# Local attention and a gated projection on one core: every engine's work put into one written list of 919 pieces

## Chip, core and metric

The kernel runs on one core of a Trainium2 chip. A core has a matrix engine (PE, whose weight loads are listed apart as PEld), a vector engine (DVE), a scalar engine (ACT), a GpSimd engine (POOL) and a queue that only issues transfers here (SP). Each engine takes its own instructions strictly in the order in which the program wrote them; between engines there are semaphores. The metric is the device time of one execution in microseconds (us); the span of a profile is the part of it from the first to the last instruction.

## What is computed

`reference` works on 4 batches, 8 heads, 768 positions and a head dimension of 64. It is float32 throughout.

```python
k_sum = k.reshape(B, H, 24, 32, D).max(axis=3)
v_sum = v.reshape(B, H, 24, 32, D).mean(axis=3)
scores_l = q @ k.T / 8, kept where |i - j| < 16
scores_s = q @ k_sum.T / 8 + log(32)
a = softmax(concat(scores_l, scores_s))
x = a @ concat(v, v_sum)                  # heads side by side: B, S, 512
gate = sigmoid(sum over k of conv_w[k] * x shifted by 4 - k)
out = (gate * (x @ w_val)) @ w_out
```

So a query sees 31 neighbours and 24 block summaries; a causal convolution of five taps gates the first 512 x 512 projection, and a second one follows. The three weights come in as 64-bit floats and are made into float32 on the chip.

## The kernel before

**Tiling.** There are 12 groups g of 256 positions (three to a batch) and 24 units u, two to a group, each with four heads. A unit runs through these stages, and the letters in brackets are those that the change uses: scores on PE (`mm_s`, s), mask and row minimum on DVE (`snorm`, n), exponentials and row sums on ACT (`exps`, e), reciprocal on DVE (r) and scaling on POOL (m, both in `norm`), transposes on PE (`tp`, t), their copy on ACT (`pcopy`, c), attention output on PE (`mm_x`, x), copies to SBUF on ACT and the float32 rest on POOL (`xout`: X and Y, Z), first tap on ACT (`ginit`, I), four more taps on DVE (`taps`, T), tanh on ACT (`gate`, G). Once for each group come the projections on PE (`val_mm`, v, and `out_mm`, o), with their evacuations: gating on DVE (gf), rounding on ACT (gh), rest on POOL (gl), output copy on ACT (ob) and store (O). From group 1 on the projections run as three passes, high and low parts of operand and weight; group 0 runs in one float32 pass straight from the tile `wf`, for which all four row blocks of a weight must be converted.

**Weights.** Each of the eight row blocks of `w_val` and `w_out` is converted by an ACT pass (L212, rb), a DVE shift (L220, sh) and a DVE shift-and-or (L221, or), then split by ACT (L252, wc) and POOL (L253, wl). Both weights pass through the one tile `wf`.

**Buffers.** PSUM holds one score buffer of two banks, one bank each for transposes, attention output and gate, and three banks of tag `pp` that projections and block summaries share. Queries have two tiles (`qbd`, L87 to 91), keys two tiles to each of four tags, `v` two tiles. Batch 0's raw values sit in key tiles.

**Order.** The schedule is manual: each engine's queue is the program text. Setup and units 0 to 7 are written out by hand (L611 to L791): two to three units of attention, then group 0's projection, and so on. From unit 8 on `step(s)` (L560) repeats one pattern: a projection, x of unit s-2, s and n of unit s, t of unit s-1, the exponentials, taps of unit s-2, a second projection. Loads are issued at fixed steps (`LOAD_K`, `LOAD_VT`, `early_loads`, `late_loads`); `fill_vs` (L193) copies block sums into a loaded `v` tile with four transfers.

Of the kernel before, what the change touches and what calls it, by code (L numbers as in the profile page):

```python
# [21 lines left out]
QT = 64  # L22
# [23 lines left out]
LOADS = "k0 q0 m k1 q1 n0 i k2 q2 n1 k3 q3 n2 n3 v0 c Q w0 w1 w2 w3 v1"  # L46
UPB = NTH * NHP
LOAD_K = {1: (2, 2, 4, 5)}
LOAD_VT = {1: (2, 2, 5, 6)}
PREP_K = {1: (-1,) * 4}  # L50
PREP_V = {1: (-1,) * 4}
DVE_V = ((1, 3),)
for _b in range(2, B):
    LOAD_K[_b] = tuple(_b * UPB + w for w in (-5, -4, -3, -2))
    LOAD_VT[_b] = LOAD_K[_b]
    PREP_K[_b] = tuple(_b * UPB + w for w in (-3, -2, -1, 0))
    PREP_V[_b] = tuple(_b * UPB + w for w in (-4, -3, -2, -1))
# [3 lines left out]
def tile_attention_then_gated_conv(  # L61
# [25 lines left out]
    NQB = 2  # L87
    qbd = []
    for i in range(NQB):
        t = cpool.tile([P, NPR, SG], F32, tag=f"qbd{i}", name=f"qbd{i}")  # L90
        qbd.append(t)
# [52 lines left out]
    def prep_v(b, pr):  # L144
        t = wk.tile([P, NB], F32, tag="vsT", name=f"vsT_{b}_{pr}", bufs=4)
# [80 lines left out]
    wraw = {}  # L226

    def load_w(nm, src, k, pool, tag):
        raw = pool.tile([P, 2 * DM if wide else DM], U32, tag=tag, name=f"raw_{nm}{k}")
        nc.sync.dma_start(raw, src[k * P : (k + 1) * P, :].bitcast(U32))  # L230
        wraw[nm, k] = raw

    wf = cpool.tile([P, 4, DM], F32, tag="wf", name="wf")

    scaled = {}

    def pre_w(nm, k):
        if wide:
            scaled[nm, k] = rebias(wraw[nm, k], DM, f"{nm}{k}", 2)

    def conv_w(nm, k):
        st = wf[:, k]
        raw = wraw.pop((nm, k))
        if wide:
            to_f32(st, raw, DM, f"{nm}{k}", 2, scaled.pop((nm, k), None))
        else:
            nc.vector.tensor_copy(st, raw.bitcast(F32))

    def split_w(nm, k):
# [29 lines left out]
    for a in LOADS.split():
        acts[a[0]](int(a[1]) if len(a) > 1 else 0)  # L280
# [6 lines left out]
    def group(g):  # L287
        if g not in grp:
            grp[g] = dict(
                xh=wk.tile([P, NPR, SG], F32R, tag="xh", name=f"xh_{g}") if g else None,  # L290
                xl=wk.tile([P, NPR, SG], F32R, tag="xl", name=f"xl_{g}") if g else None,
                gt=wk.tile([P, NPR, SG], F32, tag="gt", name=f"gt_{g}"),
                xf=wk.tile([P, NPR, HALO + SG], F32, tag="xf", name=f"xf_{g}"),
            )
            halo = grp[g]["xf"][:, :, :HALO]
            if g % NTH == 0:
                nc.gpsimd.memset(halo, 0.0)
            else:
                nc.gpsimd.tensor_scalar(
                    halo, grp[g - 1]["xf"][:, :, SG:], 1.0, 1.0, ALU.mult, ALU.mult  # L300
                )
        return grp[g]

    def mm_s(u, r):
        b, th, hp = units[u]
        g = b * NTH + th
        if r == 0:
            st[u] = dict(
                sp=ps_s.tile([P, 2, 512], F32, tag="s", name=f"s_{u}"),
                sn=wk.tile([P, NP, KW], F32, tag="sn", name=f"sn_{u}"),  # L310
                p=wk.tile([P, NP, KW], F32, tag="p", name=f"p_{u}", bufs=3),
                nm=wk.tile([P, NP], F32, tag="nm", name=f"nm_{u}", bufs=4),
                rs=wk.tile([P, NP], F32, tag="rs", name=f"rs_{u}", bufs=4),
            )
        pr = 2 * hp + r
        for j in range(TPU // 2):
            for e in range(2):
                for h in range(2):
# [4 lines left out]
                        st[u]["sp"][64 * e : 64 * e + 64, h, c * KW : c * KW + KW],  # L323
                        qbd[g % NQB][64 * h : 64 * h + 64, pr, i * QT : i * QT + QT],
# [5 lines left out]
    def snorm(u, r):  # L330
        b, th, hp = units[u]
        s = st[u]
        for j in range(TPU // 2):
            for h in range(2):
# [5 lines left out]
                    s["sn"][:, n, :],  # L340
                    s["sp"][:, h, c * KW : c * KW + KW],
# [5 lines left out]
                    s["nm"][:, n : n + 1],  # L347
                )

    def exps(u, r):  # L350
        s = st[u]
        for n in range(TPU * r, TPU * r + TPU):
            nc.scalar.activation(  # L353
                s["p"][:, n, :], s["sn"][:, n, :], AF.Exp, bias=s["nm"][:, n : n + 1],
                scale=-1.0, accum_out=s["rs"][:, n : n + 1],
            )

    def norm(u):
# [4 lines left out]
        for r in range(2):
            w = slice(TPU * r, TPU * r + TPU)
            nc.gpsimd.tensor_tensor(  # L365
                s["p"][:, w],
                s["p"][:, w],
                ri[:, w].unsqueeze(2).broadcast_to([P, TPU, KW]),
                ALU.mult,
            )  # L370
# [499 lines left out]
```

## Time and profile before

| | |
|---|---|
| runs, us | 262.33, 264.52, 330.56; median 264.52 |
| profiled span, us | 258.7 |
| span to the fastest run | 3.6 us lie around it |
| busy, us | PE 228.9, DVE 187.4, ACT 193.0, POOL 151.5 |
| first matmul starts, last one ends | 5.48, about 255.1 us |

Busy times overlap a little within an engine, as an instruction starts before the one ahead has quite ended, so the distance between starts is the better price of a piece. PE's sum is also swollen where it runs at the lower clock.

### The profile page before, as it was taken

What the parts mean: (1) busy time and instruction counts of PE and PEld (TensorE: products, weight loads), DVE (VectorE), ACT (ScalarE), POOL (GpSimd) and SP (SyncE); (2) the same over time, 40 slices, a digit from 0 to 9 for tenths busy, and PEclk for the clock granted to TensorE, in tenths of its full rate; (3) what the DMA queues carried; (4) which work ended last, traced back from release to release, by engine and by line L of the source; (5) the groups of instructions that cost most, each with busy time, mean ns of one, the idle gap of its engine ahead of it and who ended that gap; (6) DMA issues with size and microseconds to landing.
All of it is one profiled execution on the core that took longest, in us unless ns stands there. A gap on an engine that the chain in (4) does not pass through costs nothing.

```text
span 258.7 us, 7312 instructions
## 1 busy us (share of the span) xinstructions
PE 228.9 (88%) x2652; PEld 193.3 (75%) x2652; DVE 187.4 (72%) x691; ACT 193.0 (75%) x619; POOL 151.5 (59%) x212
## 2 busy tenths in 40 slices
PE   1258996997496979999999999999999999999994
PEld 1146785953392969888988988898889888988982
DVE  1856899999983877779777867987696669645610
ACT  1548997977829499888987898899879888976311
POOL 2243087769818297878664788897446634655130
PEclk9999999999977699999999999999999999999999
DMA  6999989284413968617118989172065323110122
GB/s 193 398 403 412 340 299 393 33 319 164 130 50 46 331 210 307 211 38 263 44 16 225 387 252 383 35 249 82 5 202 181 113 97 71 42 43 0 44 81 81
DMA packets 16884, 46.39 MB, mean 179 GB/s; under 512 B 2352, under 2 KB 3120, under 8 KB 16848
## 3 DMA queue, kind: packets, MB, share of 16 engines
q1 hardware_dynamic: 16848, 45.93, 51.7%
q8 instruction: 21, 0.34, 0.6%
q14 instruction: 15, 0.12, 0.2%
HBM read 37.46 MB, written 6.29 MB: 169 GB/s over the span
## 4 chain that ended last, share of the span: by engine, by line
PE 70%; DVE 13%; ACT 8%; POOL 3%; DMA 2%; issue 2%; SPq 1%; DVEq 0%; ACTq 0%; POOLq 0%
PE out L502 24%; PE val L464 21%; PE s L322 8%; PE x L398 8%; PE pt L378 8%; DVE g L439 5%; ACT p L353 4%; DVE sn L339 3%; DMA vT<-in_vT_dram 2%; DVE wf L221 1%; POOL p L365 1%; DVE wf L220 1%; DVE ks L129 1%; POOL wo L253 1%; ACT pts L382 1%
## 5 line engine op out<-in xcount | busy, mean ns | idle before, releaser
L439 DVE SCALAR_TENSOR_TENSOR g<-xf,cwt,g 128x256 f32<-128x256 f32 x192 | 93.9, 489 | 13.1 <-ACT g L430 6.0
L353 ACT ACTIVATE p<-sn,nm 128x120 f32<-128x120 f32 x192 | 73.3, 388 | 9.7 <-DVE nm L339 9.7
L365 POOL TENSOR_TENSOR p<-p,ri 128x480 f32<-128x480 f32 x48 | 47.0, 1001 | 41.2 <-DVE ri L362 37.6
L339 DVE CUSTOM_DVE_ANT_0 sn<-s,mask 128x120 f32<-128x120 f32 x192 | 40.9, 278 | 32.4 <-PE s L322 32.3
L464 PE MATMUL val<-xh,wv 128*128 128x256 f32 x352 | 51.1, 287 | 0.0
L502 PE MATMUL out<-wo,gh 128*128 128x512 f32 x176 | 46.8, 406 | 1.4 <-POOL wo L253 1.4
L464 PEld LDWEIGHTS val<-xh,wv 128*128 128x128 f32 x352 | 45.4, 191 | 0.3 <-issue 0.2
L322 PE MATMUL s<-k,qbd 64*64 64x120 f32 x768 | 28.9, 289 | 13.8 <-POOL k L139 11.1
L416 POOL TENSOR_TENSOR xl<-xf,xh 128x512 fp32r<-128x512 f32 x22 | 28.4, 1291 | 19.0 <-ACT xf L414 14.3
L378 PE MATMUL pt<-ident,p 128*120 128x128 f32 x192 | 31.6, 289 | 7.9 <-ACT pts L382 4.5
L502 PEld LDWEIGHTS out<-wo,gh 128*128 128x128 f32 x176 | 31.5, 188 | 8.5 <-POOL wo L253 2.1
L353 ACT ACTIVATION_READ_ACCUMULATOR p<-sn,nm 128x1 f32 x192 | 37.0, 193 | 0.0
L382 ACT COPY pts<-pt 120x512 f32<-120x512 f32 x48 | 27.6, 575 | 10.2 <-PE pt L378 10.2
L398 PEld LDWEIGHTS x<-pts,v 120*64 120x64 f32 x768 | 27.2, 141 | 10.1 <-issue 7.0
L322 PEld LDWEIGHTS s<-k,qbd 64*64 64x64 f32 x768 | 21.7, 143 | 17.4 <-POOL k L139 15.3
L487 POOL TENSOR_TENSOR gl<-gf,gh 128x512 fp32r<-128x512 f32 x22 | 28.5, 1298 | 7.9 <-ACT gh L478 7.9
L398 PE MATMUL x<-pts,v 120*64 120x64 f32 x768 | 31.2, 229 | 1.9 <-ACT pts L382 0.7
L378 PEld LDWEIGHTS pt<-ident,p 128*120 128x120 f32 x192 | 21.7, 142 | 14.4 <-POOL p L365 6.7
L447 ACT ACTIVATE gt<-g 128x512 f32<-128x512 f32 x24 | 14.3, 598 | 22.9 <-DVE g L439 22.9
L464 PE MATMUL val<-xl,wv 128*128 128x256 f32 x176 | 28.4, 283 | 0.0
L153 POOL TENSOR_TENSOR vT<-vT 128x384 f32<-128x384 f32 (+3 forms) x44 | 25.7, 584 | 2.6
L502 PE MATMUL out<-wo,gl 128*128 128x512 f32 x88 | 25.4, 409 | 0.7 <-POOL gl L487 0.7
(51 smaller groups left out, 270.3 us busy)
## 6 DMA issues: line engine op xcount, KB each, us to landing
v<-in_vw_dram SPq DMA_DIRECT2D x24, 512.0 KB
k<-in_kT_dram SPq DMA_DIRECT2D x16, 478.0 KB
vT<-in_vT_dram SPq DMA_DIRECT2D x16, 384.0 KB
out_dram<-ob SPq DMA_DIRECT2D x24, 256.0 KB
qbd<-in_qT_dram SPq DMA_DIRECT2D x11, 512.0 KB
raw_wv<-in_wv_dram SPq DMA_DIRECT2D x4, 512.0 KB
raw_wo<-in_wo_dram SPq DMA_DIRECT2D x4, 512.0 KB
v<-vs SPq DMA_DIRECT2D x36, 48.0 KB
```

What stands on the lines that cost most here:

```text
L322: nc.tensor.matmul(st[u]["sp"][64 * e : 64 * e + 64, h, c * KW : c * KW + KW], qbd[g % NQB][64 * h : 64 * h + 64, pr, i * QT : i * QT + QT ...
L339: nc.vector.tensor_tensor_reduce(s["sn"][:, n, :], s["sp"][:, h, c * KW : c * KW + KW], mask[:, mv, :], -1.0 / math.sqrt(D), 3.0e38, ALU.a ...
L353: nc.scalar.activation(s["p"][:, n, :], s["sn"][:, n, :], AF.Exp, bias=s["nm"][:, n : n + 1], scale=-1.0, accum_out=s["rs"][:, n : n + 1],)
L365: nc.gpsimd.tensor_tensor(s["p"][:, w], s["p"][:, w], ri[:, w].unsqueeze(2).broadcast_to([P, TPU, KW]), ALU.mult,)
L378: nc.tensor.transpose(s["pt"][:KW, i, :], s["p"][:, TPU * r + i, :], ident)
L382: nc.scalar.copy(s["pts"][:, TPU * r : TPU * r + TPU], s["pt"][:KW])
L398: nc.tensor.matmul(dst, v[:KW, i, c0 : c0 + D], src, start=True, stop=g > 0)
L416: nc.gpsimd.tensor_tensor(G["xl"][:, prs, :], x[:, prs, HALO:], G["xh"][:, prs, :].bitcast(F32), ALU.subtract)
L439: nc.vector.scalar_tensor_tensor(gt[:, r], x[:, pr, o : o + SG], cwt[:, pr, o : o + 1], gt[:, r], ALU.mult, ALU.add,)
L464: nc.tensor.matmul(pp[:, r], w, x, start=(n == 0), stop=(n == len(terms) - 1))
L487: nc.gpsimd.tensor_tensor(G["gl"][:, cos, :], gf, G["gh"][:, cos, :].bitcast(F32), ALU.subtract)
L502: nc.tensor.matmul(pp, x, w, start=(n == 0), stop=(n == len(terms) - 1))
```

## The change

The functions that issued several engines' work are cut up, so that each piece is one engine's work on one half unit, one projection half, one weight block or one transfer. The loops over steps and the hand-written beginning are gone; one list names all 919 pieces in program order, and each engine's queue is that list's part for it. No arithmetic changes and no instruction is added or dropped. Tile counts stay, except that the queries take their two tiles from the rotating pool, so a query load can take either tile once it is free. A projection of values is cut into halves r that can stand apart. `DVE_COPY` and `POOL_LOW` are empty. In the list, `s6.1` is unit 6, half 1; `v1.0.1` is group 1, pair 0, half 1; `Lk`, `Lq`, `Lv`, `Lu`, `Lwv`, `Lwo` are loads of keys, queries, values, transposed values and weight blocks, and F is `fill_vs`.

```diff
-LOADS = "k0 q0 m k1 q1 n0 i k2 q2 n1 k3 q3 n2 n3 v0 c Q w0 w1 w2 w3 v1"
-    LOAD_K[_b] = tuple(_b * UPB + w for w in (-5, -4, -3, -2))
...
+RAW_TAG = {'wv': ['gh', 'gl', 'gh', 'gl'], 'wo': ['gh', 'gl', 'xh', 'xl']}
+BUFS = {'p': 3, 'nm': 4, 'pts': 2, 'sn': 2, 'xh': 2, 'xl': 2, 'gt': 2, 'xf': 2, 'gf': 3, 'gh': 2, 'gl': 2, 'ob': 2, 'sc': 2, 'ks': 2, 'vsT': 4, 'rs': 4}
+ORDER = """
+Lk0.0 Lk0.1 ks0.0 ks0.1 Lp0 Lp1 Lc Lm Lk0.2 shc kc0.0 Lp2 kc0.1 s0.0 Lk0.3 Ln0 n0.0 e0.0 ks0.2
+kc0.2 cv s0.1 n0.1 ks0.3 s1.0 Lq1 Lp3 Ln2 e0.1 kc0.3 vp0.0 n1.0 Ln1 Li Ln3 s1.1 r0 vp0.1 Lwv2
+Lwv1 m0.0 vc0.1 n1.1 m0.1 e1.0 e1.1 rbc s2.0 vp2.1 s2.1 Lwv3 Lq2 vp1.0 vp1.1 Lk1.1 t0.0 n2.0
+Lk1.0 Lv0 Lwo3 Lu1.0 n2.1 s3.0 s3.1 c0.0 vp2.0 vp3.1 r1 n3.0 vp3.0 n3.1 shwv3 e2.0 e2.1 m1.1
+shwv2 m1.0 vc3.1 t0.1 c0.1 vc0.0 t1.1 vc1.0 s4.0 s4.1 hal0 vc2.1 vc3.0 vc2.0 vc1.1 rbwv3 r2
+rbwv2 e3.0 vb0 c1.1 vb1 orwv2 n4.0 n4.1 ks1.1 shwv1 ks1.0 m2.1 t1.0 vbc0 e3.1 Lv1 s5.0 vbc1 s5.1
+wcwv2 rbwv1 x0.0 x0.1 n5.1 orc orwv3 n5.0 orwv1 e4.0 Y0 c1.0 Lwv0 Lq3 r3 I0 T0.0 t2.1 e4.1 c2.1
+rbwv0 x1.0 m2.0 kc1.0 tv1.0 m3.0 kc1.1 x1.1 wcwv3 shwv0 r4 t2.0 s6.0 orwv0 c2.0 s6.1 t3.0 T0.1
+Lk1.2 Lu1.2 Lwo1 F1 Lwo2 Lk1.3 Y1 wlwv2 m3.1 Lv2 Lu1.3 rbwo3 c3.0 wcwv1 n6.0 Lq7 G0 ks1.2 I1
+v0.1.0 v0.0.0 x2.0 T1.0 ks1.3 x2.1 t3.1 e5.0 m4.0 T1.1 wcwv0 e5.1 tv1.2 wlwv3 kc1.2 Y2 rbwo2
...
+m9.0 I7 Z7 o1.1 m10.1 t9.0 c9.0 O0.1 Lu2.0 Lq6 n11.0 F4 Lk3.1 O1.0 Lu2.3 T7.0 v3.0.0 n11.1
+v3.0.1 x8.0 T7.1 kc2.1 m9.1 tv2.0 m10.0 ks2.2 x8.1 Lv5 t9.1 e11.0 gh2.1 X8 Y8 c9.1 v3.1.0 gl2.0
+hal4 kc2.3 Z8 e11.1 G7 s12.0 s12.1 v3.1.1 n12.0 n12.1 t10.0 I8 gf3.0 x9.0 T8.0 x9.1 e12.0 kc2.2
+gl2.1 s13.0 X9 e12.1 s13.1 Y9 gh3.0 c10.0 n13.0 n13.1 o2.0 t10.1 gf3.1 r11 T8.1 s14.0 s14.1
+e13.0 ob2.0 G8 c10.1 I9 n14.0 r12 n14.1 o2.1 tv2.3 m11.0 m11.1 vsp2 t11.0 ob2.1 Lq8 F5 hal5
...
+"""
-    qbd = []
-    for i in range(NQB):
...
+    def qt(g):
+        if g not in qtile:
+            qtile[g] = ld.tile([P, NPR, SG], F32, tag="q", name=f"q_{g}")
+        return qtile[g]
...
-    prep_k(0, 0)
-    mm_s(0, 0)
...
-    for s in range(8, NU + 2):
-        step(s)
...
+    for word in ORDER.split():
+        nm_ = word.rstrip("0123456789.")
+        ops[nm_](*(int(a) for a in word[len(nm_) :].split(".") if a))
```

## Rows read from the trace of the kernel before

**Rows 1.** The page: granted clock, DMA and GB/s in 40 slices of 6.47 us.

```profile
PEclk9999999999977699999999999999999999999999
GB/s 193 398 403 412 340 299 393 33 319 164 130 50 46 331 210 307 211 38 263 44 16 225 387 252 383 35 249 82 5 202 181 113 97 71 42 43 0 44 81 81
```

**Rows 2.** The chain that ended last, in order of time: start, us, what.

```profile
99.10 2.91 PE val L464 x24
102.00 0.44 PE pt L378 x4
102.44 2.80 PE out L502 x12
105.24 1.08 PE x L398 x32
106.32 0.98 PE s L322 x32
107.88 2.83 PE val L464 x24
...
255.10 0.60 ACT ob L509
```

**Rows 3.** Busy time by stretch: us, then PE, PEld, DVE, ACT, POOL; clock, DMA, GB/s.

```profile
5.48:30.20 24.72, 15.39 (x280) 12.00 (x280) 17.31 (x73) 15.75 (x57) 6.75 (x20) 1.00 1.03 403
30.20:98.44 68.24, 56.99 (x610) 44.35 (x604) 56.84 (x186) 52.27 (x168) 46.75 (x61) 0.92 0.59 200
98.44:234.00 135.56, 135.56 (x1640) 119.29 (x1638) 104.48 (x417) 115.59 (x382) 91.24 (x121) 1.00 0.46 152
```

**Rows 4.** PE's order of time: start, us, what, idle before it and its releaser.

```profile
5.48 1.08 PE L322 MATMUL s<-k,qbd 64*64 64x120 f32 x16 [5.48 <-POOL k L139]
...
30.24 7.17 PE L464 MATMUL val<-xf,wf 128*128 128x256 f32 x32
...
51.84 3.59 PE L502 MATMUL out<-wf,gf 128*128 128x512 f32 x8
```

**Rows 5.** DVE's order of time, the same columns.

```profile
3.97 0.95 DVE L129 TENSOR_REDUCE ks<-k 128x24 f32<-128x768 f32 x1 [3.97 <-DMA k<-in_kT_dram]
...
26.40 0.28 DVE L339 CUSTOM_DVE_ANT_0 sn<-s,mask 128x120 f32<-128x120 f32 x1 [1.15 <-PE s L322]
...
28.03 0.42 DVE L220 TENSOR_SCALAR wf<-raw_wv 128x512 uint32<-128x512 uint32 x1
...
32.33 4.11 DVE L439 SCALAR_TENSOR_TENSOR g<-xf,cwt,g 128x256 f32<-128x256 f32 x8
...
53.62 1.76 DVE L129 TENSOR_REDUCE ks<-k 128x24 f32<-128x768 f32 x2
```

**Rows 6.** Groups of DVE by line: busy us, mean ns, idle before and its releaser.

```profile
L471 DVE SCALAR_TENSOR_TENSOR gf<-gt,val 128x512 f32<-128x512 f32 x24 | 15.7, 657 | 2.4 <-PE val L464 2.4
L361 DVE TENSOR_SCALAR ri<-rs 128x8 f32<-128x8 f32 x24 | 6.2, 256 | 4.8 <-ACT p L353 4.7
L362 DVE RECIPROCAL ri<-ri 128x8 f32<-128x8 f32 x24 | 4.9, 203 | 0.8
L173 DVE TENSOR_REDUCE vpad<-vT 128x12 f32<-128x384 f32 x8 | 4.0, 546 | 0.7 <-DMA vT<-in_vT_dram 0.7
```

**Rows 7.** Lines 220 and 221 (ns min/median/max), and POOL's next work after 23 us.

```profile
L220 DVE TENSOR_SCALAR wf<-raw_wv x4: 414/420/423, 22.9 to 29.2; 128x512 uint32<-128x512 uint32 x4
L220 DVE TENSOR_SCALAR wf<-raw_wo x4: 416/1048/1359, 36.7 to 52.2; 128x512 uint32<-128x512 uint32 x4
L221 DVE SCALAR_TENSOR_TENSOR wf<-sc_wo,wf x4: 692/992/1561, 38.0 to 52.7; 128x512 uint32<-128x512 uint32 x4
30.07 0.38 POOL L299 TENSOR_SCALAR xf<-xf 128x16 f32<-128x16 f32 x1 [7.07 <-ACT xf L414]
```

**Rows 8.** DVE's busy time in two stretches of the beginning.

```profile
0.00:60.00 60.00, 46.88 (x165) 1.00 0.85 310
60.00:100.00 40.00, 29.65 (x107) 0.87 0.49 158
```

More of the change, by code (lines that the diff above doesn't have):

```diff
@@ L304, in mm_s, with part @@
-    def mm_s(u, r):
[L305 to L314, printed above, removed]
+    def part(kind, g, shape, dt=F32):
+        key = kind, g
+        if key not in grp:
+            grp[key] = wk.tile(shape, dt, tag=kind, name=f"{kind}_{g}", bufs=BUFS[kind])
+        return grp[key]
@@ new lines, in of, with attn, sn, pr_ @@
+    def of(u):
+        b, th, hp = units[u]
+        return b, th, hp, b * NTH + th
+    def attn(kind, u, shape):
+        key = kind, u
+        if key not in st:
+            st[key] = wk.tile(shape, F32, tag=kind, name=f"{kind}_{u}", bufs=BUFS[kind])
+        return st[key]
+    def sn(u):
+        return attn("sn", u, [P, NP, KW])
+    def pr_(u):
+        return attn("p", u, [P, NP, KW])
+    def nm(u):
+        return attn("nm", u, [P, NP])
+    def rs(u):
+        return attn("rs", u, [P, NP])
@@ L315, in mm_s, with pts, bank, sp @@
+    def pts(u):
+        return attn("pts", u, [KW, NP, P])
+    def bank(pool, tag, u, shape):
+        key = tag, u
+        if key not in st:
+            st[key] = pool.tile(shape, F32, tag=tag, name=f"{tag}_{u}")
+        return st[key]
+    def sp(u):
+        return bank(ps_s, "s", u, [P, 2, 512])
+    def xp(u):
+        return bank(ps_x, "x", u, [P, 2, SG])
+    def gp(u):
+        return bank(ps_g, "g", u, [P, 2, SG])
+    def mm_s(u, r):
+        b, th, hp, g = of(u)
         pr = 2 * hp + r
@@ L362, in norm, with recip @@
+                scale=-1.0, accum_out=rs(u)[:, n : n + 1],
+            )
+    def recip(u):
+        ri = st["ri", u] = wk.tile([P, NP], F32, tag="ri", name=f"ri_{u}", bufs=4)
+        nc.vector.tensor_scalar(ri, rs(u), 1e-9, None, ALU.add)
         nc.vector.reciprocal(ri, ri)
[L363 to L370, printed above, removed]
+    def norm(u, r):
+        w = slice(TPU * r, TPU * r + TPU)
+        nc.gpsimd.tensor_tensor(
+            pr_(u)[:, w],
+            pr_(u)[:, w],
+            st["ri", u][:, w].unsqueeze(2).broadcast_to([P, TPU, KW]),
+            ALU.mult,
+        )
@@ L481, in tile_attention_then_gated_conv, with taps @@
-    lows = []
-    def val_low():
-        while lows:
-            g, cos, gf = lows.pop(0)
-            G = group(g)
-            nc.gpsimd.tensor_tensor(
-                G["gl"][:, cos, :], gf, G["gh"][:, cos, :].bitcast(F32), ALU.subtract
-            )
+            src = xf(g)[:, pr, HALO:] if u in LATE_INIT else xp(u)[:, r]
+            nc.scalar.activation(gp(u)[:, r], src, AF.Copy, scale=cwt[:, pr, NK - 1 : NK])
+    def taps(u, r):
+        b, th, hp, g = of(u)
+        pr = 2 * hp + r
+        for o in range(NK - 1):
+            nc.vector.scalar_tensor_tensor(
+                gp(u)[:, r], xf(g)[:, pr, o : o + SG], cwt[:, pr, o : o + 1], gp(u)[:, r],
+                ALU.mult, ALU.add,
+            )
@@ new lines, in gate, with val_mm @@
+    def gate(u):
+        b, th, hp, g = of(u)
+        nc.scalar.activation(gt(g)[:, two(hp), :], gp(u), AF.Tanh, scale=0.5)
+    def val_mm(g, cp, r):
+        wh, wl = wsplit["wv"][:, :, 0], wsplit["wv"][:, :, 1]
+        if ("val", g, cp) not in pss:
+            pss["val", g, cp] = ps_p.tile([P, 2, SG], F32, tag="pp", name=f"val_{g}_{cp}")
+        pp = pss["val", g, cp]
+        cs = slice((2 * cp + r) * P, (2 * cp + r) * P + P)
+        if g in FP32_G:
+            terms = [(wf[:, ci, cs], xf(g)[:, ci, HALO:]) for ci in range(4)]
+        else:
+            terms = [(w[:, ci, cs], xh(g)[:, ci, :]) for ci in range(4) for w in (wh, wl)]
+            terms += [(wh[:, ci, cs], xl(g)[:, ci, :]) for ci in range(4)]
+        for n, (w, x) in enumerate(terms):
+            nc.tensor.matmul(pp[:, r], w, x, start=(n == 0), stop=(n == len(terms) - 1))
@@ new lines, in gated, with g_head, g_rest @@
+    def gated(g, cp):
+        gf = grp["gf", g, cp] = wk.tile(
+            [P, 2, SG], F32, tag="gf", name=f"gf_{g}_{cp}", bufs=BUFS["gf"]
+        )
+        nc.vector.scalar_tensor_tensor(
+            gf, gt(g)[:, two(cp), :], 1.0, pss.pop(("val", g, cp)), ALU.add, ALU.mult
+        )
+    def g_head(g, cp):
+        nc.scalar.copy(gh(g)[:, two(cp), :], grp["gf", g, cp])
+    def g_rest(g, cp):
+        nc.gpsimd.tensor_tensor(
+            gl(g)[:, two(cp), :], grp["gf", g, cp], gh(g)[:, two(cp), :].bitcast(F32), ALU.subtract
+        )
@@ L491, in out_mm @@
     def out_mm(g, si):
-        G = group(g)
         wh, wl = wsplit["wo"][:, :, 0], wsplit["wo"][:, :, 1]
-        pp = ps_p.tile([P, DM], F32, tag="pp", name=f"out_{g}_{si}")
+        pp = pss["out", g, si] = ps_p.tile([P, DM], F32, tag="pp", name=f"out_{g}_{si}")
         rows = slice(si * P, si * P + P)
         if g in FP32_G:
-            terms = [(G["gf", ci // 2][:, ci % 2, rows], wf[:, ci, :]) for ci in range(4)]
+            terms = [(grp["gf", g, ci // 2][:, ci % 2, rows], wf[:, ci, :]) for ci in range(4)]
```

676 lines of the change are left out of this document (198 added, 478 removed).

## Prediction, made before the changed kernel was built

> **What bounds the kernel now.** I read four views in this order: the busy shares by stretch, the chain that ended last, each engine's order of time over the first 100 us, and the groups by line for prices. By stretch [rows 3], PE is busy 135.56 us of 135.56 between 98.44 and 234, at full clock, while DVE, ACT and POOL have room (104.5, 115.6 and 91.2 us). The chain [rows 2] says the same in pieces: one step of the loop is PE alone, value projection 2.91, transposes 0.44, output projection 2.80, attention output 1.08, scores 0.98, transposes again, and 8.78 us after it began the next starts. So nothing can be won there but by giving PE less to do, which the change doesn't. What can be won lies before 98.44.
>
> How much, I get by pricing PE's whole work. A unit costs about 8.75 us, so the 22 units of groups 1 to 11 cost 192.5. Group 0 costs 22.5: its projections 7.0 and 2 x 3.6 [rows 4], its attention output with two matmuls in place of one 4 x 1.08, scores 2.0 and transposes 2.0. The transposes of block sums add 2.2. Sum 217.2. PE starts at 5.48 [rows 4] and ends at 255.1 [rows 2]: 249.6 us for 217.2 of work, 32.4 lost. After 98.44 there are only some 1.5 of them, so 31 us are lost in the first 98, where the weights are still being loaded and converted, PE waits for units that aren't ready, and in three slices the granted clock falls to 0.6 or 0.7 [rows 1]. The mean clock of 0.92 over 68.24 us [rows 3] says that some 5.5 of the 31 are the clock's, whose two levels are 1.2 and 2.4 GHz.
>
> **The change part by part.** No instruction is added or removed, so the sum of each engine stays, and the whole question is when PE gets its work. The list starts with attention alone: 14 score halves, 7 transposes halves and units 0 and 1's outputs stand before the first projection half `v0.1.0`, against four units' scores and two outputs before it in the old order. Afterwards scores run about five units ahead of the group that is projected. I look for the latest handover to PE: time at which it can happen, plus all of PE's work behind it.
>
> First handover, `v0.1.0`. It needs all four row blocks of the first weight in float32, the last by the DVE piece `orwv0`. Two things bound that. Transfers: the list puts 11.46 MB up to and with that block (four key and four padded value loads, queries, three weight blocks, two keys of batch 1, two value tiles and so on, sizes from the shapes). The old order moved 6.47 us x (193 + 398 + 403 + 412 + 340) GB/s = 11.3 MB by 32.3 us [rows 1], so the block lands at about 32.6, and behind it stand a shift 0.42, a reciprocal 0.46 and a shift-and-or 0.69 [rows 6, 7]: not before 34.2. DVE itself: up to `orwv0` it has 12 mask pieces at 0.815 (eight in 26.40 to 28.03 are two units' halves) [rows 5] = 9.8, 6 key maxima at 0.88 [rows 5] = 5.3, 8 block sums, 4.0 in all [rows 6], 5 reciprocals at 0.46 = 2.3, four conversions at 0.42 + 0.69 = 4.4, one taps piece 2.06 [rows 5] and the taps' own weights about 1: 28.9, from 3.97 on [rows 5], so 32.9 without a wait. I add 2.6 of waits (for scores and loads; the old order had 1.15 at one such place [rows 5]) and 1.1 for the port below: 36.6. That is 6 us later than the old 30.24 [rows 4], but with 15.6 us of PE's work done in place of about 11. PE then has 217.2 - 15.6 = 201.6 left. Were it never held again, PE would end at 238.2 and the span at 241.8, as 3.6 lie between PE's end and the span's [rows 2].
>
> Second handover, `o2.0`. PE reaches it 60.1 us of work later, at 96.7. The three `pp` banks are then held by `o1.1`, whose output copy stands far back on ACT, and by the two value projections of group 3, so `o2.0` needs the bank that the DVE piece `gf3.0` sets free. DVE's part up to there: 16 taps pieces at 2.06 (eight instructions take 4.11, a piece is four) = 33.0; 26 mask pieces = 21.2; 12 key maxima = 10.6; 8 block sums 4.0; 7 gatings at 0.66 = 4.6; 11 reciprocals at 0.46 = 5.1; eight conversions at 1.11 = 8.9; two single pieces, some 1.9 [rows 5 to 7]. Sum 89.3, of which 60.4 come after `orwv0`. With 3.6 for the port and 2.5 for waits on ACT between taps (I and G stand between two units' taps) it ends at 36.6 + 66.5 = 103.1. DVE is later than PE by 6.4, and decides. Behind `o2.0` PE has 32 value halves at 1.43 (45.9), 28 attention halves at 0.54 (15.1), 27 transposes at 0.51 (13.8), 20 score halves at 0.49 (9.8), 20 output tiles at 2.80 (56.0) and two block transposes (0.9): 141.5. With 0.5 for later holds PE ends at 245.1, the span at 248.7.
>
> Later handovers have room: gatings of groups 3 to 6 come 5 to 16 us of DVE's work ahead of PE's need by the same sums, since DVE is the less loaded engine from there on [rows 3]. Their cost is taken as 0.5; if that cover goes, each such hold costs what DVE is late, up to 4 us in all. The tail is as before: output copy and store behind the last tile.
>
> **The port.** The old order converted the first weight while POOL was idle for 7.07 us, and each shift took 0.42; those of the second weight, with POOL at work, took 0.42 to 1.36, median 1.05, and the joins 0.69 to 1.56 [rows 7]. With means near 0.97 and 1.06 that is 0.91 lost for a block, 3.6 for four. The list now has POOL scale probabilities and add value trees while the first weight is converted, so the price lies between 3.6 (second weight alone) and 7.3 (both alike); below 3.6 I see no reason. I take 4.7, nearer to the first, since POOL is still half idle at 20 to 30 us. The Trainium skill ("SBUF — State Buffer", section "Who interferes with whom") speaks against the change here: it says that such a DVE instruction and a GpSimd one that reads SBUF exclude each other, the later one being blocked until the other ends. The trace's spread from 0.42 to 1.36 agrees. By that rule taken at its worst, each of 16 instructions would wait out most of a POOL instruction and the sum would be some 5 us higher.
>
> **Transfers and waits that move.** SP's queue is reordered too. Query load 7 goes out ahead of 4 to 6 and keeps one of two tiles until unit 15, so loads 4, 5 and 6 can start only when the unit before has left the other tile. PE's work between is 8 us for load 5 (`t6`, both tiles of group 0's output, `t7`) and 10 for load 6; the first key load, of like size, took at most 4 us from the start of everything [rows 5]. For load 4 there are only 4.4 us, but PE is then waiting for DVE anyway. I cost it at 0; if its cover goes, 1 to 3 us. `F4` stands behind load 6 and could be 1 us late: in the 0.5.
>
> **Rivals.** (a) *DVE is never late*: the port costs what it did and ACT answers in time. PE goes from the first handover on without a hold, span 241.8, and 239.5 with the transfers' bound of 34.2. For it: DVE's sum leaves `gf3.0` at 93.3 with no wait at all, ahead of PE. Against it: no stretch of the old beginning had DVE that full. (b) *DVE stays as full as it was*: in the first 60 us it was busy 46.88 of the 56.0 after its start [rows 8], 0.84. Then 89.3 us of pieces take 106.3, `o2.0` starts at 110.3 and the span is 110.3 + 141.5 + 0.5 + 3.6 = 255.9. For it: a tighter weave of four queues gives every late piece more to hold up; a fall of the clock as in slices 12 to 14, 5.5 us, would end in the same place. (c) *Slower*: the in-order weave starves DVE. From 60 to 100 us the old kernel had it at 29.65 of 40 [rows 8], 0.74, because taps waited for ACT and masks for PE; the new list has such crossings from the start. At 0.74 the pieces take 120.7, `o2.0` starts at 124.7, the span is 270.3. The mechanism costs more than the change gives from the point where `o2.0` starts later than 258.7 - 3.6 - 0.5 - 141.5 = 113.1. Against it: the list sets other work between a unit's last taps and the next one's first. (d) *It doesn't run ahead*: loads or the three banks hold the front back to the old two units and the time stays near 258.7; the list's order leaves little room for that.
>
> **How the numbers follow.** The sum stands against the profiled execution: span 258.7, and about 3.6 around it by the fastest run, 262.3; the median of the three runs is 2.2 above that. The forecast span of 248.7 is then 252.3, say 252. Rivals in the same measure: (a) 243 to 245.4, (b) 259.5, (c) 273.9, (d) about 262. Chances: forecast 0.45, (a) 0.20, (b) 0.19, (c) 0.11, (d) 0.05. The range that holds the time 8 times in 10 goes from (a)'s lower end, 243, to 262, beyond (b); the forecast alone has 248 to 256. Two per cent, about what a measurement of this kernel can tell from no change, is 5.2 us. Faster by more: the forecast, (a) and a fourth of (b), 0.70; within: the rest of (b), (d): 0.18; slower: (c) and a little, 0.12.
>
> **What would show it.** Right: first projection half at 35 to 38 us; `o2.0` at 100 to 106, held by DVE; PE without gaps from there; conversions of the first weight longer than 0.42. Wrong: `o2.0` after 113; PE waits of more than 5 us after it; a granted clock below 0.9 over a long stretch; or PE waiting for transfers, which would put the bound at SP's queue.

## The result: 249.88 us, as forecast, but not by the forecast's steps

The changed kernel took 249.88 us, median of 4 runs (249.72 to 251.77); the kernel before took 264.02 beside it. The ratio is 0.956, 95% interval 0.948 to 0.963; it counts fast executions alone, so it leaves out the 330.56 us that one run of the kernel before took and isn't the quotient of the two medians. A second time (the run called "The new list again" below) it took 249.46 against 262.09: 0.951, 0.945 to 0.957. The forecast was 252.0, faster.

The profiled execution has a span of 248.2 us, against 248.7 forecast. Its page answers [rows 1].

```profile
PEclk9999989999999999999999999999999999999998
GB/s 217 395 408 408 407 357 351 238 270 302 156 100 258 233 221 239 110 113 354 115 182 161 245 207 64 245 119 26 177 46 81 207 118 3 85 45 42 3 85 86
```

Its busy times by stretch answer [rows 3, 8], with the same columns; the last two rows are DVE alone.

```profile
3.50:39.81 36.31, 24.88 (x389) 20.24 (x389) 29.71 (x137) 25.31 (x100) 18.79 (x38) 0.95 1.01 378
39.81:244.33 204.52, 202.46 (x2266) 174.83 (x2264) 156.15 (x555) 164.38 (x518) 132.52 (x171) 1.00 0.48 155
...
0.00:60.00 60.00, 48.93 (x200) 0.97 0.93 340
60.00:100.00 40.00, 38.36 (x141) 1.00 0.62 197
```

The three slices at 0.6 to 0.7 are gone; one at 0.8 is left, from 31 to 37 us. From the first projection half at 39.81 to PE's end at 244.33, PE is busy 202.46 of 204.52 us at a granted clock of 1.00. DVE is busy 38.36 us of 40 between 60 and 100; before it was 29.65.

PE's own order, to be held against [rows 4]:

```profile
7.02 1.08 PE L433 MATMUL s<-k,q 64*64 64x120 f32 x16 [7.02 <-DMA q<-in_qT_dram]
...
33.38 0.62 PE L484 MATMUL pt<-ident,p 128*120 128x128 f32 x4 [1.77 <-POOL vT L209]
34.15 0.34 PE L501 MATMUL x<-pts,v 120*64 120x64 f32 x4
...
35.79 0.52 PE L501 MATMUL x<-pts,v 120*64 120x64 f32 x4
...
39.81 3.62 PE L559 MATMUL val<-xf,wf 128*128 128x256 f32 x16
...
64.40 7.03 PE L587 MATMUL out<-wf,gf 128*128 128x512 f32 x16
...
82.90 0.73 PE L587 MATMUL out<-wo,gl 128*128 128x512 f32 x2 [0.37 <-POOL gl L573]
...
101.36 2.12 PE L587 MATMUL out<-wo,gh 128*128 128x512 f32 x8
```

The first projection half comes at 39.81 and the first tile `o2.0` at 101.36, with no idle time named before it. By the same sums as before, PE takes 237.3 us (7.02 to 244.33, where the last output copy can start) for 217.2 of work: 20.1 lost in place of 32.4. Of these, 17.2 lie ahead of 39.81 (32.8 us for 15.6 of work) and 2.9 behind it.

DVE's conversions by line, 282 (shift) and 286 (join), answer [rows 7].

```profile
L282 DVE TENSOR_SCALAR wf<-raw_wv x4: 417/423/698, 23.5 to 36.2; 128x512 uint32<-128x512 uint32 x4
L282 DVE TENSOR_SCALAR wf<-raw_wo x4: 415/420/1053, 49.7 to 62.0; 128x512 uint32<-128x512 uint32 x4
L286 DVE SCALAR_TENSOR_TENSOR wf<-sc_wv,wf x4: 639/659/725, 24.5 to 37.9; 128x512 uint32<-128x512 uint32 x4
L286 DVE SCALAR_TENSOR_TENSOR wf<-sc_wo,wf x4: 679/1024/1779, 50.1 to 64.0; 128x512 uint32<-128x512 uint32 x4
```

In DVE's order of time, the last join of each weight, and the piece `gf3.0`:

```profile
37.91 0.64 DVE L286 SCALAR_TENSOR_TENSOR wf<-sc_wv,wf 128x512 uint32<-128x512 uint32 x1
...
62.30 2.38 DVE L286 SCALAR_TENSOR_TENSOR wf<-sc_wo,wf 128x512 uint32<-128x512 uint32 x2
...
99.51 0.68 DVE L565 SCALAR_TENSOR_TENSOR gf<-gt,val 128x512 f32<-128x512 f32 x1
```

The first weight is ready at 38.55, the second at 64.68, about when PE arrives (`o0.1` starts at 64.40). `gf3.0` ends at 100.19, 1.2 us before `o2.0` starts: DVE doesn't hold that tile.

### The profile page after: what moved, and what is told of

It reads as the page before. It is cut to its first block, busy times and chain, and to the rows that moved or that the text cites. A ratio compares the mean times of both kernels' runs of the same rounds, so it can differ in the third digit from the quotient of the medians.

```text
span 248.2 us, 7306 instructions
## 1 busy us (share of the span) xinstructions
PE 227.3 (92%) x2652; PEld 195.1 (79%) x2652; DVE 185.9 (75%) x691; ACT 191.6 (77%) x619; POOL 151.5 (61%) x212
## 4 chain that ended last, share of the span: by engine, by line
PE 49%; DVE 23%; ACT 12%; POOL 5%; DMA 4%; issue 4%; SPq 1%; DVEq 0%; POOLq 0%; ACTq 0%
PE out L587 18%; PE val L559 14%; DVE g L538 12%; PE s L433 5%; PE x L501 5%; PE pt L484 5%; ACT p L462 5%; DMA k<-in_kT_dram 4%; DVE sn L449 4%; POOL p L474 2%; DVE gf L565 2%; DVE ks L181 2%; ACT g L532 2%; ACT gt L545 1%; ACT pts L491 1%
## 5 line engine op out<-in xcount | busy, mean ns | idle before, releaser
L474 POOL TENSOR_TENSOR p<-p,ri 128x480 f32<-128x480 f32 x48 | 47.8, 1002 | 29.8 <-DVE ri L470 22.2
L559 PE MATMUL val<-xh,wv 128*128 128x256 f32 x352 | 50.4, 285 | 0.0
L587 PE MATMUL out<-wo,gh 128*128 128x512 f32 x176 | 45.7, 401 | 0.0
L559 PEld LDWEIGHTS val<-xh,wv 128*128 128x128 f32 x352 | 44.4, 188 | 0.7 <-issue 0.2
L433 PE MATMUL s<-k,q 64*64 64x120 f32 x768 | 29.9, 299 | 12.3 <-DMA q<-in_qT_dram 7.0
L433 PEld LDWEIGHTS s<-k,q 64*64 64x64 f32 x768 | 23.1, 150 | 17.0 <-POOL k L195 10.1
L484 PEld LDWEIGHTS pt<-ident,p 128*120 128x120 f32 x192 | 22.7, 144 | 8.5 <-issue 2.4
L209 POOL TENSOR_TENSOR vT<-vT 128x384 f32<-128x384 f32 (+3 forms) x44 | 26.5, 603 | 4.1 <-DMA vT<-in_vT_dram 1.5
L587 PE MATMUL out<-wo,gl 128*128 128x512 f32 x88 | 24.3, 396 | 0.4 <-POOL gl L573 0.4
L559 PEld LDWEIGHTS val<-xl,wv 128*128 128x128 f32 x176 | 23.8, 188 | 0.1
```

What stands on the lines that cost most here:

```text
L433: nc.tensor.matmul(sp(u)[64 * e : 64 * e + 64, h, c * KW : c * KW + KW], qt(g)[64 * h : 64 * h + 64, pr, i * QT : i * QT + QT], ktile[b, p ...
L474: nc.gpsimd.tensor_tensor(pr_(u)[:, w], pr_(u)[:, w], st["ri", u][:, w].unsqueeze(2).broadcast_to([P, TPU, KW]), ALU.mult,)
L484: nc.tensor.transpose(pt[:KW, i, :], pr_(u)[:, TPU * r + i, :], ident)
L559: nc.tensor.matmul(pp[:, r], w, x, start=(n == 0), stop=(n == len(terms) - 1))
L587: nc.tensor.matmul(pp, x, w, start=(n == 0), stop=(n == len(terms) - 1))
```

## The experiments

Theory A: the time is that of the first projection half plus PE's whole work behind it. The runs ask whether that is so, where in the list the gain sits, and whether something can be bettered.

**The first projection later.** The last block of the first weight is converted three DVE pieces later.

```diff
-... m3.0 kc1.1 x1.1 wcwv3 shwv0 r4 t2.0 s6.0 orwv0 c2.0 s6.1 ...
+... m3.0 kc1.1 x1.1 wcwv3 r4 t2.0 s6.0 c2.0 s6.1 ...
-... n6.0 Lq7 G0 ks1.2 I1 v0.1.0 ...
+... n6.0 Lq7 G0 ks1.2 shwv0 orwv0 I1 v0.1.0 ...
```

> In the new list the DVE pieces shwv0 and orwv0, which finish the first weight's last block, are put some 4 us of DVE's work later, behind T0.1, n6.0 and ks1.2; DVE's work up to o2.0 stays the same in sum. Theory A (the first projection half starts the clock, and PE works on without a hold behind it): v0.1.0 starts at 42 to 43 in place of 39.81, and the time rises by 2 to 3 us, to about 252.5. Rival B (as predicted, DVE's sum up to gf3.0 decides at o2.0): DVE has the same work in the same time, so the time moves by less than 0.5 us.

Measured: 255.29 us (ratio to before 0.969, 0.962 to 0.976). PE's order:

```profile
42.65 5.41 PE L556 MATMUL val<-xf,wf 128*128 128x256 f32 x16 [3.31 <-DVE wf L283]
...
69.01 7.03 PE L584 MATMUL out<-wf,gf 128*128 128x512 f32 x16
...
106.85 2.12 PE L584 MATMUL out<-wo,gh 128*128 128x512 f32 x8
```

The half came 2.84 us later than in the changed kernel and the span of this profile is 6.5 longer. So the first projection does move the end, here by more than its own delay: after the wait of 3.31 its 16 matmuls took 5.41 in place of 3.62 (granted clock 0.81 from 39 to 48 us). Then the delay was 4.6 at `o0.1` and 5.5 at `o2.0`. How much more differs from execution to execution: two others have spans of 251.0 and 252.3 us, against 246.1 to 250.0 with the unchanged list.

**The new list's first part, then the old order.** Everything up to `o2.0` is as in the new list; the pieces left follow in the old order.

```diff
 ... n13.0 n13.1
-o2.0 t10.1 gf3.1 r11 T8.1 ...
+(the remaining pieces, in the old order)
```

> The new list up to the piece ahead of o2.0 (about 101 us into the span), then all that is left in the order of the kernel before. Theory A (the whole gain is made in the first 100 us, since both kernels keep PE busy after it): within 1.5 us of the new list, 249 to 251.5. Rival C (running ahead of the projections is needed as a cushion to the end): the holds come back and at least a third of the gain is lost, 254 or more.

Measured: 250.5 us, ratio 0.957 (0.953 to 0.961). The gain is made ahead of `o2.0`. PE's order there:

```profile
38.96 3.62 PE L556 MATMUL val<-xf,wf 128*128 128x256 f32 x16
...
100.92 2.13 PE L584 MATMUL out<-wo,gh 128*128 128x512 f32 x8
```

From `o2.0` to its end PE needs 144.25 us against 142.97 in the changed kernel and 142.14 in that kernel's second profile, so the new order of the rest is worth some 1 to 2 us.

**The old beginning, then the new list.** The reverse: the 311 pieces that were written out by hand stand in their old order, the rest in the new.

> The order of the kernel before for all that it wrote out by hand (up to the gate of unit 5, about 89 us into its span), then the rest in the new list's order (batch 2's loads and trees of values kept in old order, for their two tiles). Theory A: what was lost is lost, 261 to 265, as the kernel before. Rival C: a good part of the gain comes in the later part, 257 or less.

Measured: 272.08 us, ratio 1.041 (1.036 to 1.046), which neither theory gave. PE's order, and then its stretch from 79 to 92:

```profile
91.31 1.88 PE L430 MATMUL s<-k,q 64*64 64x120 f32 x32 [11.40 <-DVE nm L446]
```
```profile
79.00:92.00 13.00, 1.60 (x48) 1.40 (x49) 7.19 (x27) 8.81 (x33) 9.27 (x11) 0.68 0.60 190
```

At the joint PE stands 11.40 us at unit 9's scores, since unit 8's masks are behind the old part's taps on DVE, these behind exponentials on ACT, and PE's queue has no projection ahead of them. This says nothing of running ahead as such; it shows what one bad joint in an in-order list costs.

**One wait of the old order removed.** In the old order, unit 7's scores waited 2.63 us for key block sums (70.41). On the changed code, with the old order as its list, two of these and POOL's copies of them are moved forward.

```diff
-DVE:  ... T3.0 ... ks1.2 ... ks1.3 ...
+DVE:  ... ks1.2 ks1.3 T3.0 ...
-POOL: ... m6.0 ... kc1.2 ... kc1.3 ...
+POOL: ... kc1.2 kc1.3 m6.0 ...
```

> The whole order of the kernel before, with one thing moved: the maxima ks1.2 and ks1.3 go ahead of unit 3's taps on DVE, and kc1.2 and kc1.3 ahead of unit 6's scaling on POOL, so that unit 7's scores needn't wait 2.63 us for them. If the wait alone cost time: 262 to 263, some 2 us less than before. If the fall of the granted clock behind that wait (0.6 to 0.7 in three slices) came from it, the clock's 5 us go too: 257 to 259. If the wait is only handed on to the next late piece: no change, 264.

Measured: 259.29 us, ratio 0.992 (0.988 to 0.995), which in spans is 258.7 to 257.3. PE's order:

```profile
68.06 1.05 PE L430 MATMUL s<-k,q 64*64 64x120 f32 x32 [0.27 <-POOL k L192]
...
76.84 0.73 PE L584 MATMUL out<-wo,gh 128*128 128x512 f32 x2 [0.85 <-POOL wo L321]
...
90.47 0.62 PE L481 MATMUL pt<-ident,p 128*120 128x128 f32 x4 [1.93 <-ACT pts L488]
```

The wait fell to 0.27, but PE only got sooner to the next ones. Unit 7's scores came 2.35 earlier than in the kernel before, the end 1.4. So this wait alone isn't what the old beginning loses. The next run gives the same code without this edit.

**The old order as a list.** A control: the changed code, the old order in its list.

> The changed code with the old order written as its list: the same 919 pieces, each engine's queue as it was. Theory A (only the order of the pieces changes the time): the time of the kernel before, within 1 us, first projection half at 30 us. Rival D (part of the gain comes from the cut functions or from the query tiles that rotate): 1 to 4 us less than before.

Measured: 264.22 us, ratio 1.012 (1.009 to 1.015). Theory A missed by 3 us, and rival D has the sign wrong too. One stretch, then PE's order:

```profile
93.00:102.00 9.00, 7.37 (x54) 5.71 (x58) 4.33 (x11) 5.33 (x20) 5.57 (x8) 0.62 0.46 134
```
```profile
22.10 1.11 PE L481 MATMUL pt<-ident,p 128*120 128x128 f32 x4 [0.36 <-POOL p L471]
...
28.48 0.34 PE L498 MATMUL x<-pts,v 120*64 120x64 f32 x4 [0.53 <-ACT g L529]
```

Up to 20.4 us the two profiles agree within 0.1 us. Then the transposes at 22.1 took 1.11 us against 0.65 before, and the attention output at 28.48 came 1.62 later. In 93 to 102 us the granted clock was 0.62; before it was 1.00 there. So the same pieces in the same order took longer on PE. The 1.62 us at the beginning aren't the code's own: the run with the keys moved has the same code and, up to some 60 us, the same queues, and there the two came as in the kernel before:

```profile
22.07 0.65 PE L481 MATMUL pt<-ident,p 128*120 128x128 f32 x4 [0.93 <-POOL p L471]
...
26.88 0.34 PE L498 MATMUL x<-pts,v 120*64 120x64 f32 x4 [0.53 <-ACT g L529]
```

The five transposes of block sums at 20.4 took 0.77 us in that run and in the kernel before, 1.33 in this control and in the old beginning with the new list behind it. So PE's slow beginning lasted longer in two of the four profiles; why it did is not known. The rest of the 3 us stays open, and with it whether the order alone is worth some 12 us (against the kernel before) or 15 (against this control).

The control also changes what the moved keys are worth: against it their span is 5.5 us shorter, not 1.4. Of this 1.6 lie ahead of the edit; behind it the granted clock of 68 to 106 us was 0.91 with the keys moved, 0.82 in the control and 0.87 in the kernel before. Whether the edit or chance kept the clock higher, one profile of each can't tell.

**The bank of `o2.0`.** The output copy `ob1.1` and its store go right behind `e11.0` on ACT, so that `o2.0` doesn't need the bank of `gf3.0`.

```diff
-... x8.1 Lv5 t9.1 e11.0 gh2.1 ...
+... x8.1 Lv5 t9.1 e11.0 ob1.1 O1.1 gh2.1 ...
-... ob1.1 ... O1.1 ...
```

> Only output copy ob1.1 and its store move, to right behind ACT's e11.0, so that o2.0 finds a free bank without gf3.0. Theory A (PE reaches o2.0 by itself, DVE is not late there): same as the new list, 249 to 250 us on a chip where before is 261 to 264, within 0.3, and o2.0 within 0.3 of 101.4. The prediction's theory (o2.0 is held by DVE's gf3.0): 1 to 6 us less.

Measured: 248.8 us, ratio 0.954 (0.950 to 0.958). PE's order:

```profile
37.98 3.72 PE L556 MATMUL val<-xf,wf 128*128 128x256 f32 x16 [0.29 <-DVE wf L283]
...
54.99 1.05 PE L430 MATMUL s<-k,q 64*64 64x120 f32 x32 [0.40 <-DMA q<-in_qT_dram]
...
100.16 2.12 PE L584 MATMUL out<-wo,gh 128*128 128x512 f32 x8
```

From the first projection half to `o2.0` PE needed 62.18 us; in the unchanged list's second profile below it is 37.93 to 100.12, 62.19. The bank was no hold. The expected 101.4 for `o2.0` fell for another reason: the half itself came 1.83 earlier, as it also did with the unchanged list.

**The new list again.** Unchanged, as a base for the last three runs.

> The new list unchanged, beside the two runs below on one chip: 248.5 to 250 us where before is 261 to 264. Theory C (which of the two clock levels the first 40 us get differs between executions) also has v0.1.0 anywhere from 38 to 40 by the profile, as the run with ob1.1 early already had it at 37.98.

Measured: 249.46 us, as above. PE's order, then the last output copy on ACT:

```profile
6.18 1.08 PE L433 MATMUL s<-k,q 64*64 64x120 f32 x16 [6.18 <-DMA q<-in_qT_dram]
...
37.93 3.72 PE L559 MATMUL val<-xf,wf 128*128 128x256 f32 x16 [0.39 <-DVE wf L286]
...
63.29 7.03 PE L587 MATMUL out<-wf,gf 128*128 128x512 f32 x16
...
100.12 2.14 PE L587 MATMUL out<-wo,gh 128*128 128x512 f32 x8
```
```profile
242.26 0.60 ACT L593 ACTIVATE ob<-out 128x512 f32<-128x512 f32 x1 [2.19 <-PE out L587]
```

The same kernel has its first projection half at 37.93 here and at 39.81 in its other profile. 0.84 of the difference is the first score (6.18 against 7.02, the query load). Most of the rest is the clock: from 34 to 37 us it was granted at 0.64 there, and sets of four matmuls took 0.52 us in place of 0.34.

**Three tries to start the projection earlier.** In the first, c1.0, Y0 and I0 go ahead of `e4.0` on ACT, c2.0 behind Y1, and the last block's load, shift and join go forward.

```diff
-ACT: ... vbc1 wcwv2 rbwv1 e4.0 Y0 c1.0 I0 e4.1 c2.1 rbwv0 wcwv3 c2.0 Y1 ...
+ACT: ... vbc1 c1.0 wcwv2 rbwv1 Y0 I0 rbwv0 e4.0 e4.1 c2.1 wcwv3 Y1 c2.0 ...
-DVE: ... orwv1 r3 T0.0 shwv0 r4 orwv0 ...
+DVE: ... orwv1 shwv0 orwv0 r3 T0.0 r4 ...
```

> New list with three local moves ahead of the first projection: unit 1's copy c1.0, unit 0's output copy and first tap before unit 4's exponentials on ACT; c2.0 and t3.0 behind Y1; the last block of the first weight loaded one place earlier, with its shift and join before r3 and T0.0 on DVE. Theory A (the first projection's start is what PE's end follows from): v0.1.0 at 37 to 38 in place of 39.8, time 1 to 3 us below the new list's. Rival E (the second weight's conversions on DVE are a handover just as tight, o0.1 starts where they end): v0.1.0 as early, but o0.1 still at 64 and the time within 0.5 us of the new list's.

Measured: 250.56 us, ratio 0.960 (0.958 to 0.963), and the half at 39.48. DVE was done with the weight at 34.5, but PE waited 2.05 us for ACT's copy `c2.1`, behind both halves of `e4`. DVE and ACT are equally late here, and easing one shows the other. As the half didn't move, rival E was not tested.

The second try moves `c2.1` between the halves; it also lets `wcwv2` and `wcwv3`, roundings of the first weight for which PE has no early use, stand back on ACT.

```diff
-ACT: ... c1.0 wcwv2 rbwv1 Y0 I0 rbwv0 e4.0 e4.1 c2.1 wcwv3 Y1 c2.0 rbwo3 c3.0 ...
+ACT: ... c1.0 rbwv1 Y0 I0 rbwv0 e4.0 c2.1 e4.1 Y1 c2.0 rbwo3 c3.0 wcwv2 wcwv3 ...
```

> As the run with three local moves, with the copy that held the first projection there (c2.1, behind both halves of unit 4's exponentials) put between them, and two roundings of the first weight later on ACT; nothing behind the first projection is moved. All theories: v0.1.0 at 37 to 38, with no wait of 2 us before it. Rival E (the second weight's joins on DVE are as tight a handover): o0.1 waits 1 to 2 us for them, o0.1 stays at 64 to 64.7 and the time is within 0.7 us of the new list's. Theory A (PE's end follows from the first projection alone): o0.1 at 62 to 63 and 1.5 to 2.5 us less than the new list.

Measured: 253.12 us, ratio 0.967 (0.961 to 0.972). POOL's order, then PE's, with the same columns:

```profile
39.44 1.27 POOL L321 TENSOR_TENSOR wv<-wf,wv 128x512 fp32r<-128x512 f32 x1 [3.38 <-ACT wv L317]
...
50.32 1.18 POOL L192 COPY k<-ks 128x84 f32<-128x84 f32 x2
```
```profile
51.56 0.64 PE L430 MATMUL s<-k,q 64*64 64x120 f32 x16 [2.20 <-POOL k L192]
...
55.32 0.51 PE L556 MATMUL val<-xl,wv 128*128 128x256 f32 x2 [1.36 <-POOL xl L517]
```

The half came at 38.06, no earlier than in the unchanged list, and `o0.1` came at 66.89, 3.6 later than there: 2.20 and 1.36 us of waits. The rounding that PE didn't need held POOL for 3.38 us, and with it the key sums for unit 7, which stand behind the weight's low part on POOL (50.32; 46.41 in the unchanged list).

The third try puts only these two roundings back.

```diff
-ACT: ... c1.0 rbwv1 Y0 I0 rbwv0 e4.0 c2.1 e4.1 Y1 c2.0 rbwo3 c3.0 wcwv2 wcwv3 ...
+ACT: ... c1.0 wcwv2 rbwv1 Y0 I0 rbwv0 e4.0 c2.1 e4.1 wcwv3 Y1 c2.0 rbwo3 c3.0 ...
```

> As the front run, with the two roundings of the first weight on ACT put back to where the new list has them (wcwv2 right behind c1.0, wcwv3 behind e4.1). If those were what cost the front run its time (POOL stood 3.4 us before the low part of block 2, and key block sums and low parts behind it came some 4 us later): the waits of 2.20 us at unit 7's scores and 1.36 at the first low-part matmuls go, o0.1 at 62.5 to 64, time within 1 us of the new list's 249.5. Theory A beyond that: v0.1.0 at 36.5 to 37.5 and up to 1 us less than the new list; rival E (the second weight's joins): o0.1 held by DVE at 63 to 64.5 and no gain.

Measured: 249.39 us, ratio 0.953 (0.948 to 0.959). PE's order:

```profile
38.32 0.65 PE L481 MATMUL pt<-ident,p 128*120 128x128 f32 x4 [1.31 <-ACT pts L488]
38.81 3.62 PE L556 MATMUL val<-xf,wf 128*128 128x256 f32 x16
...
63.42 0.65 PE L481 MATMUL pt<-ident,p 128*120 128x128 f32 x4
63.90 7.03 PE L584 MATMUL out<-wf,gf 128*128 128x512 f32 x16
```

The wait of 2.20 is gone, that of 1.36 is 0.19, and the time is that of the unchanged list: the cause of the 3.7 us is shown. The half came at 38.81, now behind ACT's `c2.0`, and `o0.1` started at 63.90, about when DVE's last join ended (63.97). PE was busy right up to `o0.1`, as in the two profiles of the unchanged list, and its 16 matmuls took 7.03 in each, so the joins held it in none of them. A PE that came earlier might be held: that part of rival E stays untested.

**More moves behind the first projection.** One run adds to the first try an earlier second weight, earlier roundings and low parts of group 1, and `ob1.1` early.

```diff
-DVE: ... shwo0 T2.0 r6 T2.1 n8.0 n8.1 shwo1 orwo0 orwo1 r7 gf1.0 T3.0 T3.1 n9.0 n9.1 ...
+DVE: ... shwo0 r6 n8.0 n8.1 shwo1 orwo0 orwo1 T2.0 T2.1 r7 n9.0 n9.1 gf1.0 T3.0 T3.1 ...
-ACT: ... rbwo1 G2 c6.1 I3 c6.0 e8.0 X5 wcwo1 wcwo3 Y5 G3 I4 ob0.1 e9.0 c7.0 gh1.0 ...
+ACT: ... rbwo1 c6.1 c6.0 e8.0 G2 I3 X5 wcwo1 wcwo3 Y5 gh1.0 G3 I4 ob0.1 e9.0 c7.0 ...
-POOL: ... gl1.0 tv2.1 gl1.1 ...
+POOL: ... gl1.0 gl1.1 tv2.1 ...
```

> As the run with the three local moves, and besides: on DVE the second weight's last conversions and unit 8's masks stand before unit 2's taps; on ACT the copies and roundings of group 1's gating come earlier, the low part of it on POOL before the value tree; ob1.1 right behind e11.0. Theory A with two handovers: v0.1.0 at 37 to 38, o0.1 at 61.5 to 62.5, o1.0 without its wait of 0.4, time 2 to 3.5 us below the new list's. Rival E': taps that start later make the next units' gating late, o1.0 or o2.0 wait for it and the gain is under 1 us.

Measured: 257.59 us, ratio 0.990 (0.983 to 0.997). PE waited 1.72 us at `o0.0` for `gf1.0`, whose bank it needs, and 3.75 for POOL's scaling ahead of the transposes at 88.65; the granted clock from 84 to 97 was 0.74. E' had the kind of hold right, not its size: it is a loss against the unchanged list, not a small gain.

Another adds a milder form to the second try, with `ob1.1` early.

```diff
-DVE: ... T2.0 r6 T2.1 n8.0 n8.1 shwo1 orwo0 orwo1 r7 gf1.0 ...
+DVE: ... T2.0 r6 n8.0 n8.1 shwo1 orwo0 orwo1 T2.1 r7 gf1.0 ...
-ACT: ... Y4 e7.1 c5.1 rbwo0 rbwo1 G2 c6.1 I3 c6.0 e8.0 ...
+ACT: ... Y4 rbwo0 rbwo1 e7.1 c5.1 c6.1 c6.0 G2 I3 e8.0 ...
```

> The same front, and for the second weight: its last shift and joins on DVE before T2.1, their ACT passes before unit 7's second exponentials; ob1.1 early. If rival E holds for the run above, this one takes the gain: o0.1 at 62 to 63, 1 to 2.5 us less than the new list. Against it: T2.1 and with it gf1.0 come later, o0.0 waits for the bank and the gain is under 0.7.

Measured: 253.9 us, ratio 0.970 (0.965 to 0.975). It has the same POOL hold as the second try (2.17 us at unit 7's scores), so it tells nothing of the second weight. No version beat the changed kernel by more than its own runs differ.

## Why the prediction came out

**What bounds.** Right, as long as no new wait and no fall of the clock comes behind the first projection half. PE's end follows it by 204.52 us in the changed kernel, 204.33 in its second profile, 204.41 with `ob1.1` early and 204.75 in the third try. It isn't a law: the distance is 205.48 in the first try, 208.18 with the first projection later, where the clock fell behind the half, and 209.0 in the second try, with its waits of 2.20 and 1.36. The sum of PE's work behind it was 201.6: 2.9 us, 1.4%, too low, with 0.5 of holds foreseen.

**First handover, 36.6.** Too early: 39.81 and 37.93 in two profiles. DVE's pieces took 29.0 us from start to start, the port's price among them, where the sum had 28.9 and 1.1; the added 2.6 us of waits was the term that was mis-sized. Up to 39.9 us DVE waited 0.17 and 1.49 for loads after its start, 3.4 for PE's scores (five times) and 0.4 for ACT: 5.5. With 3.97 + 29.0 + 5.5 it ends at 38.5; the trace has 38.55. In the first profile PE came later still: its transposes waited 1.77 at 33.38, and four matmuls took 0.52 in place of 0.34 behind it. That ACT is as late as DVE I had not reckoned.

**Second handover, 103.1, held by DVE.** Wrong: this is the step that failed. PE reached `o2.0` at 101.36, and with a free bank it came no sooner. I added 6.1 us for port and waits to DVE's 60.4 behind `orwv0`, 66.5 in all; from 38.55 to the end of `gf3.0` at 100.19 are 61.6. The port came out as put (below). DVE waited only 0.6 us of the 2.5, and the pieces without the port took some 57.5 in place of 60.4: I had priced taps, gatings and conversions by their durations, whose ends overlap the next start (a taps piece of 2.06 starts at 38.47, the next piece at 40.44, 1.97 later), and the reciprocals by a mean that already held some of the port. Rival (a), *DVE is never late*, describes the mechanism; its spans of 239.5 to 241.8 failed because the first handover came later and the work behind it was 2.9 longer. The span of 248.7 is right by luck: 3.2 too little at the first handover, 2.9 too little of work and 6.4 too much of a hold cancel. Of the signs named, `o2.0` came in its range, but without the hold; the half came after 38 in one of the two profiles; and of the first weight's four shifts one was longer than 0.42.

The forecast time has a wrong term besides: it adds 3.6 us around the span, from the fastest of the three runs before. In every later run, of either kernel, time and span of one execution differ by 1.7 to 1.9 us (249.98 and 248.2 for the profiled one). With 1.8 a span of 248.7 is 250.5.

**The port.** The size was right, the instructions that pay it only in part. Three of the first weight's shifts kept 0.42, the fourth took 0.70; its joins stayed at 0.64 to 0.73, though POOL was at work: 0.3 us in all, where 1.1 were put ahead of the first handover. For the second weight, one shift of 1.05, joins of 1.36 and the pair of 2.38 cost some 2.3 above 0.42 and 0.68, against 3.6. What I had not counted is the reciprocal's first instruction, 0.16 us at its shortest. Ahead of the last join it took 0.95 beside POOL's scaling:

```profile
36.56 1.17 POOL L474 TENSOR_TENSOR p<-p,ri 128x480 f32<-128x480 f32 x1
36.81 0.95 DVE L469 TENSOR_SCALAR ri<-rs 128x8 f32<-128x8 f32 x1
```

It ends 0.03 us behind POOL's instruction, and so do those of 0.44 at 49.08 and 1.01 at 89.49. With a shorter one (0.23 at 83.59) they lost 0.8 us ahead of the first handover and 1.2 behind it, so the port's two parts come to 1.1 and 3.5, against 1.1 and 3.6; that the sums fit is chance. The Trainium skill ("SBUF — State Buffer", section "Who interferes with whom") calls the shared port an exclusive lock. These common ends and the spread to 1.78 us agree; the 5 us more that the prediction worked out as its worst case were not reached.

**Transfers.** Right at 0 in the two profiles of the changed kernel: after the first score no query load held PE, though load 7 keeps one of the two tiles until unit 15. But load 4, which the prediction hid behind a wait of PE for DVE, is on the edge. With the same queues up to there, PE waited 0.78 us for it (55.62) in the run with the new list's first part and 0.40 (54.99) with `ob1.1` early.

**Rivals.** (b) and (c) put DVE at 0.84 and 0.74 busy from its start to `gf3.0`; from 3.97 to 100 us it was busy 87.3 of 96.0, 0.91 (before, 76.5 [rows 8]). The fall of the clock that (b) counted on didn't come behind the first projection. (d) is refuted by the order of PE.

## What to carry to other kernels

Price the bound engine's whole work, and look for the last handover that it can't avoid: here the time was that point plus a constant, in four profiles within 0.5 us, and up to 4.7 us more where a later wait or a slower clock came in. Price the other engines' pieces from start to start, not by duration. When you then add waits to another engine's sum, take them from where it has waited, first loads and first results, not from a stretch in which it already runs ahead. In an in-order list, ask of a piece moved back not who reads it but what is queued behind its reader: a rounding that nobody needed cost 3.7 us by way of POOL's queue.

## What was not expected of the hardware

- A wait of PE can cost more than its length. After 3.31 us of it the next 16 matmuls took 5.41 us in place of 3.62; around a wait of 2.69 us in the old list's control (93 to 102 us) the granted clock was 0.62. After the 11.40 us at the joint, 32 score matmuls took 1.88 in place of 1.05. It needn't: behind the 2.20 us of the second try (51.56) the transposes took 0.65 and eight projection matmuls 1.19, as elsewhere at a granted clock of 1.00.
- In the first 25 us the same forms take nearly twice as long as later (32 score matmuls 1.88 at 19.47 and 1.05 at 28.41 in the changed kernel), although the granted clock of 7 to 25 us reads 1.00. The row of the clock doesn't show that beginning.
- The profile named POOL as releaser of the transposes at 33.38, but the piece before them in the bank was ACT's copy `c1.0`, which ended at 33.28, 0.1 us earlier: the single transposes' bank, not POOL, fits. In the first try, where `c1.0` goes earlier, no wait for that POOL piece is left.
